# Decode attention over a 65,536-row cache: the first 192 rows of the last V tile in three pieces instead of four

## The chip, the cores and the metric

The kernel runs on one core of a Trainium2 chip. The metric is the device time of one execution in microseconds. All times inside an execution are counted from the first instruction of its profiled span. The engines are called as in the profile: PE multiplies matrices (PEld loads its weights), DVE works on vectors, ACT computes functions such as exp, POOL serves here mostly as a hand that passes signals on, and SP issues nearly all loads.

## The reference

There is one query row for each of 32 heads, and 8 key/value heads of 65,536 rows with 128 numbers each, all in bf16. Four query heads share one key/value head.

```python
B, Hq, Hkv, Sq, Sk, D = 1, 32, 8, 1, 65536, 128
def reference(q, k, v):
    rep = Hq // Hkv
    k = jnp.repeat(k, rep, axis=1)
    v = jnp.repeat(v, rep, axis=1)
    scale = D ** -0.5
    scores = jnp.einsum("bhqd,bhkd->bhqk", q, k) * scale
    p = _softmax(scores, axis=-1)
    return jnp.einsum("bhqk,bhkd->bhqd", p, v)
```

K and V are 134 MB each and every number of them is used once (for four query heads). The result is tiny.

## The kernel before

**Tiles.** Each head's K and V are cut into two halves of 256 rows per partition (NT = 256, 128 partitions): a half is a tile of 128 x 256 rows of 128 numbers, 8.4 MB. `buf` is a ring with room for three tiles. One "row" below means one row in each of the 128 partitions, 32 KB in all.

**Loads.** SP issues the loads in the order of the list `tiles` (L153 to L156): both K halves of a head, then V halves of earlier heads, and at the very end the second V half of head 6 and both V halves of head 7. Before each load SP waits until the tile that had the same place in the ring is used up. Most tiles are one load. Head 7's K tiles and the last V tiles are cut into pieces with a semaphore for each piece: `BY` gives the pieces of three V tiles, and `PIECES` those of the very last one, (head 7, second half), in which this case's change lies. All loads stand on one queue and are worked off in order. L134 is the issue in the helper `load`.

**K and scores.** DVE transposes each half of a K tile in place (`turn`, L318). PE multiplies it with the queries into four banks of `sc` (block `scores`, L460). DVE takes the maximum, ACT the exponential (L244), and DVE transposes the weights into `Ew` (L323).

**V and sums.** PE's block `values` (L479 to L492) works on 32 rows per turn (STEP): it takes one count of the semaphore `sV` (`take`, L224: wait for one, subtract one) and issues 8 matmuls of 4 rows each into `psum_o` (L484), each with its own weights from `Ew`. The counts of `sV` are given by SP for whole tiles (L168), and for the tiles in `BY` and the first `MOVED` pieces of the last tile by POOL (L216 to L218): POOL waits for each piece's landing in order and adds the number of its turns, `n // STEP`. So a piece of 64 rows gives two turns when it has landed as a whole.

**The order on PE at the end.** After head 6's second half PE closes the sum (`summed`, L501), then runs head 7's first half (64 matmuls), goes over `values_done`, `turn` and `late`, where the number of turns for the rest of the last tile is set from `sum(PIECES[:MOVED])` (192 rows), and back into `values` for these 192 rows: 6 turns, 48 matmuls. Then it goes over `values_done` (L494 to L497) and `second_done` (L499) and branches into the block `tail` (L524).

**The tail.** The pieces behind the first `MOVED` are worked off there: the first of them (44 rows) in 11 matmuls that are spread over four column groups of the array, so that four run beside one another (L533); then `psum_o` is closed (L421), DVE picks out the sum from it (L331); meanwhile PE multiplies the last 20 rows one by one into `misc` (L542) as pieces of 8, 8 and 4 land, adds what DVE picked (L431), ACT scales it (L262) and stores it (L236). Each of these pieces has a wait of its own on PE.

Nothing waits for the matmuls of the last tile but the tail itself: no later load needs its place in the ring.

Of the kernel before, what the change touches and what calls it, by code (L numbers as in the profile page):

```python
# [24 lines left out]
N = 2  # L25
FAR = 2.0 ** 126
STEP = 32
PIECES = (64, 64, 32, 32, 44, 8, 8, 4)
MOVED = 4


@with_exitstack
def kernel(
# [19 lines left out]
    assert B_ == 1 and Sq == 1 and D_ == D and Hkv == G and Hq == G * H  # L53
    assert Sk == 2 * NT * P and sum(PIECES) == NT
    SCALE = float(D) ** -0.5
# [40 lines left out]
    def sem(name):  # L96
        sems.append(nc.alloc_semaphore(name))
        return sems[-1]
# [3 lines left out]
    sL = [sem(f"sL{x}") for x in range(sum(map(len, BY.values())))]  # L102
    sP = [sem(f"sP{x}") for x in range(len(PIECES))]
    sQ = sem("sQ")
# [27 lines left out]
    def load(at, src, s, lo=0, n=NT):  # L132
        at = at % 3 * half + lo * D
        return sp.dma_start(  # L134
            out=buf[:, at:at + n * D], in_=src[:, s * half + lo * D:s * half + (lo + n) * D]
        )
# [21 lines left out]
    for at, (kind, h, s) in enumerate(tiles):  # L158
# [16 lines left out]
        elif (h, s) == (G - 1, 1):  # L175
            lo = 0
            for n, land in zip(PIECES, sP):
                load(at, vr[h], s, lo, n).then_inc(land, 16)
# [36 lines left out]
    pool.wait_ge(vit, NT // STEP * (2 * G - 4))  # L215
    for at, (land, n) in enumerate(list(zip(sL, sum(BY.values(), ()))) + list(zip(sP, PIECES))[:MOVED]):  # L216

# [196 lines left out]
    def add(reg, n, op=ALU.add):  # L414
        pe.reg_alu(reg, reg, n, op)
# [102 lines left out]
    with block("late"):  # L518

        pe.reg_alu(r_e, r_g, 4 * (sum(PIECES[:MOVED]) - NT), ALU.mult)  # L520
        add(r_e, 2048 - 4 * G * (sum(PIECES[:MOVED]) - NT))
        pe.br("values")

    with block("tail"):  # L524
        at = sum(PIECES[:MOVED])
        left = list(zip(PIECES, sP))[MOVED:]
        own = (2 * G * 2 - 1) % 3 * half
# [60 lines left out]
```

## Time and profile before

| | us |
|---|---|
| median of three runs | 628.2 |
| lowest and highest | 627.85 and 628.54 |
| the profiled execution | 628.39 |
| its span, from the first to the last instruction | 626.5 |
| PE busy in the span | 504.5 |
| DVE busy | 331.4 |
| ACT, POOL busy | 21.1, 6.0 |
| HBM read | 268.44 MB, 429 GB/s over the span |

The span is what the rows of the trace show; the 1.9 us beside it lie before the first and after the last instruction of the program. PE's rows in order of time are matmuls, and their ends are modelled; the starts are what to go by. "Idle before" is the engine's idle time just ahead of a row, with what ended it. PEq and POOLq are the queues of the engines: the waits, register operations and branches that the engine works through between its instructions. A landing is the moment at which a load's last part is signalled; the profile gives it as time from the issue. The row PEclk and the column of that name give the clock that PE was granted, as a share of full speed.

### The profile page before, as it was taken

The numbers are of one execution on the slowest core, as the hardware profiler recorded it, in microseconds if no ns is written. First come the engines' busy times: TensorE is split into PE (matmuls) and PEld (weight loads), VectorE is DVE, ScalarE is ACT, GpSimd is POOL, SyncE is SP. The second block draws the span as 40 slices with busy tenths as digits, with TensorE's granted clock in tenths as the row PEclk, the third lists the DMA queues.
The fourth block names the chain that finished last, engine by engine and source line by source line (L and its number), as shares of the span: only waits on it lengthen the run. The fifth ranks groups of instructions, "written<-read, shape, count | busy, mean of one in ns | idle before, by whom it ended". The sixth has DMA issues, their size and how long they took to land. (4 is left out here: it accounts for less than half of the span.)

```text
span 626.5 us, 8015 instructions
## 1 busy us (share of the span) xinstructions
PE 504.5 (81%) x2186; PEld 204.2 (33%) x2186; DVE 331.4 (53%) x109; ACT 21.1 (3%) x28; POOL 6.0 (1%) x16
## 2 busy tenths in 40 slices
PE   0587299798994889948799397993979988799997
PEld 0232043243331333313333133331433333333333
DVE  3983895789214892148821588215872389410100
ACT  1000100100010000100001000010000100001000
POOL 2000000000000000000000000000000000000000
PEclk9998589799998789988899889997899998999999
DMA  9999999999999999999999999999999999999997
GB/s 371 433 469 402 469 402 469 402 460 410 452 418 423 448 402 469 402 469 402 469 402 469 402 469 402 469 402 469 402 464 406 418 425 429 435 435 435 423 431 319
DMA packets 6857, 268.46 MB, mean 429 GB/s; under 512 B 840, under 2 KB 968, under 8 KB 1224
## 3 DMA queue, kind: packets, MB, share of 16 engines
q1 hardware_dynamic: 6768, 268.44, 99.4%
q10 hardware_dynamic: 88, 0.02, 0.0%
q14 instruction: 1, 0.01, 0.0%
HBM read 268.44 MB, written 0.01 MB: 429 GB/s over the span
## 5 line engine op out<-in xcount | busy, mean ns | idle before, releaser
L318 DVE STREAM_TRANSPOSE buf<-buf 128x8192 f32<-128x8192 f32 x32 | 277.2, 8694 | 87.2 <-DVEq L224 87.2
L460 PE MATMUL sc<-buf,zeros 128*128 x1024 | 247.8, 401 | 0.0
L484 PE MATMUL psum_o<-buf,Ew 128*16 x1008 | 226.0, 382 | 11.7 <-PEq L224 11.0
L460 PEld LDWEIGHTS sc<-buf,zeros 128*128 x1024 | 102.3, 100 | 137.7 <-issue 41.6
L484 PEld LDWEIGHTS psum_o<-buf,Ew 128*16 x1008 | 89.3, 89 | 145.2 <-issue 54.9
L418 PE MATMUL sc<-zeros 128*128 128x512 bf16 x32 | 13.8, 432 | 87.8 <-PEq L224 87.8
L331 DVE TENSOR_REDUCE o_r<-psum_o 128x128 f32<-128x512 f32 x10 | 6.9, 688 | 100.2 <-DVEq L224 72.4
L327 DVE COPY o_r<-o_r 4x1 f32<-4x1 f32 x9 | 1.3, 142 | 79.7 <-DVEq L224 65.6
L418 PEld LDWEIGHTS sc<-zeros 128*128 128x128 bf16 x32 | 3.1, 98 | 97.1 <-issue 96.0
L244 ACT ACTIVATE zeros<-sc,nmb 128x2048 bf16<-128x2048 f32 x8 | 15.7, 1967 | 535.9 <-DVE nmb L382 535.9
L323 DVE STREAM_TRANSPOSE Ew<-zeros 128x1024 bf16<-128x1024 bf16 x18 | 22.3, 1240 | 14.0 <-PE psum_o L484 14.0
L504 PE MATMUL misc<-each,same 128*128 128x512 f32 x18 | 11.3, 712 | 8.6 <-PEq L224 8.6
L370 DVE TENSOR_REDUCE mx<-sc 128x1 f32<-128x2048 f32 x8 | 18.0, 2253 | 0.0
L441 PE MATMUL misc<-Ew 32*128 32x128 bf16 x1 | 0.3, 283 | 10.7 <-DVE Ew L308 10.7
L208 POOL TENSOR_TENSOR zeros<-qx,quad 128x64 bf16<-128x64 bf16 x8 | 2.4, 294 | 486.6 <-ACT o_out L251 480.4
L504 PEld LDWEIGHTS misc<-each,same 128*128 128x128 f32 x18 | 2.9, 202 | 8.9 <-issue 8.8
L421 PE MATMUL sc<-zeros 128*128 128x1 bf16 x32 | 5.2, 163 | 0.0
L418 PE MATMUL psum_o<-rows,zeros 4*128 4x512 bf16 x10 | 4.5, 451 | 0.0
L289 DVE CAST Ew<-ident 32x128 bf16<-32x128 f32 x1 | 3.0, 2984 | 2.7 <-POOL ident L193 2.7
L421 PEld LDWEIGHTS sc<-zeros 128*128 128x128 bf16 x32 | 3.0, 95 | 3.9
L251 ACT ACTIVATE o_out<-psum_f,o_r 4x128 bf16<-4x128 f32 x9 | 3.1, 345 | 29.3 <-DVE o_r L337 29.3
L431 PE MATMUL psum_f<-o_r,sel 128*4 128x129 f32 x18 | 3.9, 302 | 0.0
(32 smaller groups left out, 31.9 us busy)
## 6 DMA issues: line engine op xcount, KB each, us to landing
buf<-in_k_dram SPq DMA_DIRECT2D x8, 4096.0 KB, 28.5
buf<-in_v_dram SPq DMA_DIRECT2D x5, 4096.0 KB, 32.5
buf<-in_v_dram SPq DMA_DIRECT2D x4, 2048.0 KB, 36.4
buf<-in_v_dram SPq DMA_DIRECT2D x2, 1024.0 KB, 38.7
buf<-in_v_dram SPq DMA_DIRECT2D x1, 1408.0 KB, 42.6
buf<-in_v_dram SPq DMA_DIRECT2D x2, 256.0 KB, 40.6
buf<-in_k_dram SPq DMA_DIRECT2D x12, 34.6
buf<-in_v_dram SPq DMA_DIRECT2D x12, 34.4
```

The lines of the kernel that those rows point to most:

```text
L244: act.activation(out=E[:, :], in_=sc[:, :], func=ACT.Exp, bias=nmb[:, 0:1], scale=SCALE, accum_out=o_r[:, D:D + 1],).then_inc(exd, 1)
L251: act.activation(out=o_out[:, at:at + D], in_=psum_f[0:H, 0:D], func=ACT.Copy, scale=rl).then_inc(outs, 1)
L318: dve.transpose(out=kv, in_=kv).then_inc(kt, 1)
L323: return dve.transpose(out=Ew[:, at], in_=E[:, at])
L331: return dve.tensor_reduce(out=o_r[:, 0:D], in_=psum_o[:, :].rearrange("p (y d) -> p d y", y=4), axis=AX.X, op=ALU.max)
L370: after(dve.tensor_reduce(out=mx[:, :], in_=sc[:, :], axis=AX.X, op=ALU.max))
L418: return pe.matmul(out=bank, lhsT=lhsT, rhs=rhs, start=True, stop=False)
L421: return pe.matmul(out=bank[:, 0:1], lhsT=zer[:, 0:P], rhs=zer[:, 0:1], start=False, stop=True)
L431: return pe.matmul(out=out[0:H, 0:n], lhsT=sel[:, :], rhs=o_r[:, 0:n], start=start, stop=True)
L460: pe.matmul(out=bank, lhsT=moved(wq[:, m * SLIDE + 4 * n:][:, 0:P], slide), rhs=moved(T[:, n, m // 2, m % 2], keys), start=False, stop=False,)
L484: last = pe.matmul(out=psum_o[0:16, :], lhsT=moved(Ew[:, column(4 * j + 3):][:, 0:16], weight), rhs=moved(buf[:, 4 * j * D:][:, 0:4 * D], ...
L504: pe.matmul(out=misc[:, :], lhsT=same[:, :], rhs=each[:, :].unsqueeze(1).broadcast_to([P, 16, 32]), start=True, stop=True,).then_inc(pes, 1)
```

## The change

`PIECES` cuts the last tile's 256 rows. Its first four entries, which POOL announces and the block `values` works off, become three: 96, 64 and 32 rows instead of 64, 64, 32 and 32. Their sum stays 192 rows. `MOVED`, the number of these entries, goes from 4 to 3. The four pieces behind them, 44, 8, 8 and 4 rows, stay.

```diff
-PIECES = (64, 64, 32, 32, 44, 8, 8, 4)
-MOVED = 4
+PIECES = (96, 64, 32, 44, 8, 8, 4)
+MOVED = 3
```

By this SP issues seven loads for the tile instead of eight, POOL has three landings to pass on instead of four, with 3, 2 and 1 turns instead of 2, 2, 1 and 1, and there is one semaphore less in `sP`. PE's instructions, DVE's and ACT's are the same ones, apart from the semaphores' numbers.

## Prediction

> **What bounds the kernel now.** I read the page first: the engine shares and the forty slices, then the chain that ended last, then the order of time on PE and SP over the last 50 us, and at the end single stretches with their granted clock.
>
> ```profile
> span 626.5 us, 8015 instructions
> PE 504.5 (81%) x2186; PEld 204.2 (33%) x2186; DVE 331.4 (53%) x109; ACT 21.1 (3%) x28; POOL 6.0 (1%) x16
> PEclk9998589799998789988899889997899998999999
> DMA  9999999999999999999999999999999999999997
> HBM read 268.44 MB, written 0.01 MB: 429 GB/s over the span
> ```
>
> The DMA row is full in every slice but the last: the kernel is a stream of loads, and everything before the last tile hides under it. So the change can only be worth what it moves behind the last landings. The profiled execution took 628.39 us, 1.9 us around its span; the median of the runs is 628.2, 0.2 less. I add my difference to the median.
>
> The chain that ended last, from the issue of the pieces on (start, duration, what):
>
> ```profile
> 577.63 0.33 SPq L134
> ...
> 578.00 0.43 SPq L134
> ...
> 578.48 0.43 SPq L134
> ...
> 579.43 42.63 DMA buf<-in_v_dram
> 622.06 0.04 issue
> 622.10 0.82 PE psum_o L533 x11
> 622.92 0.11 PE psum_o L421
> 623.03 1.27 PE misc L542 x20
> 624.31 0.23 PE misc L431 x2
> 624.54 0.02 issue
> 624.56 0.36 ACT o_out L262
> ```
>
> The load issued at 579.43 is the fifth piece, 44 rows. It lands at 622.06; PE begins it 0.04 us later (L533), and from there only PE and ACT follow one another to the end. So today the stream sets the end: PE waits for the 44 rows. The question is whether PE would still be the one that waits. PE in order of time, the idle time before a row in brackets:
>
> ```profile
> 594.94 14.05 PE L484 MATMUL psum_o<-buf,Ew 128*16 x64
> 610.01 3.71 PE L484 MATMUL psum_o<-buf,Ew 128*16 x16 [1.01 <-PEq L224]
> 614.02 7.14 PE L484 MATMUL psum_o<-buf,Ew 128*16 x32 [0.30 <-PEq L224]
> 622.10 0.82 PE L533 MATMUL psum_o<-buf,Ew 128*16 128x512 bf16 x11 [0.94 <-DMA buf<-in_v_dram]
> ```
>
> PE ends the tile before at 608.99. The first piece (64 rows, 16 matmuls) starts at 610.01, pieces two to four (128 rows, 32 matmuls) run without a break from 614.02 to 621.16, and then PE has 0.94 us to spare. That is the slack in which the change must fit.
>
> **The change part by part.** *Loads.* Seven transfers instead of eight, the same 256 rows in the same order on the one queue. SP issues one transfer less; the issues lie 31 to 43 us ahead of the landings, so an earlier issue buys nothing. The landings of the first three pieces, counted from their issue at 577.63, 578.00 and 578.48:
>
> ```profile
> DMA to landing us min/median/max: 31.1/31.1/31.1
> ...
> DMA to landing us min/median/max: 35.7/35.7/35.7
> ...
> DMA to landing us min/median/max: 37.7/37.7/37.7
> ```
>
> So 64 rows are there at 608.7, 128 at 613.7 and 160 at 616.2. No row shows a 96-row transfer: its landing is bounded by these two, and I take the middle, 611.2, since the engines move the same bytes in the same order. The 44 rows come at 622.06 as before, or up to 0.1 earlier without one transfer's overhead (an estimate; it costs or gains nothing once PE is late).
>
> *Hand-over.* POOL passes a landing on through L218 and PE takes it at L224. One wait less stands on POOL; what is queued behind it there are only the same waits for later pieces. From the landing at 613.7 to PE's start at 614.02 is 0.3 us, 0.35 before rounding of the landing. So the 96 rows start at 611.2 + 0.35 = 611.55, where today 64 rows start at 610.01 and 64 more at 614.02. PE's wait grows from 1.01 to 611.55 - 608.99 = 2.55 us, in one piece.
>
> *Matmuls.* None is added or removed: 192 rows are 48 matmuls at L484. The run of 32 gives (7.14 - 0.38) / 31 = 0.218 us from start to start, 0.38 being the last one's own length. The new second piece ends where the old third one did, at 160 rows: it is there at 616.2, before PE has done 96 rows (611.55 + 24 x 0.218 = 616.8). The last 32 rows follow it some 2.5 us later (616.2 - 613.7 for 32 rows), when PE still has 64 to do, so PE runs through: the last of the 48 starts at 611.55 + 47 x 0.218 = 621.8.
>
> ```profile
> L499 PEldq COMPARE_BRANCH  x1: 213/213/213, 621.1 to 621.1; - x1
> ```
>
> *Way into the tail.* After the last matmul's start (620.78 today) PE's queue goes through L494 to L499 and branches into the block at L524. That branch begins at 621.1 and takes 0.21 us, so the tail could begin at about 621.33: 0.55 us after the last start. Today this lies under the wait for the 44 rows. After the change the tail begins at 621.8 + 0.55 = 622.35 instead of 622.10: +0.25 us, if nothing else happens. The cover of 0.94 us is gone.
>
> *The granted clock.* This is the step on which the forecast turns. The page's PEclk row has dips. Stretches of 3.41 us, laid on the edges at which the clock changes in this trace (PE, PEld, DVE, ACT and POOL busy, then clock, DMA share and GB/s):
>
> ```profile
> 37.81:41.23 3.42, 1.48 (x8) 0.57 (x6) 3.35 (x1) 0.00 (x0) 0.00 (x0) 1.00 0.91 393
> 41.23:44.64 3.41, 3.18 (x14) 1.44 (x15) 2.48 (x1) 0.00 (x0) 0.00 (x0) 1.00 1.29 557
> 222.13:225.55 3.42, 1.41 (x9) 0.53 (x7) 3.42 (x2) 0.00 (x0) 0.00 (x0) 1.00 1.33 575
> 225.55:228.96 3.41, 3.41 (x9) 1.19 (x10) 3.41 (x1) 0.00 (x0) 0.00 (x0) 0.50 0.80 346
> 228.96:232.37 3.41, 3.41 (x17) 1.52 (x16) 3.41 (x1) 0.00 (x0) 0.00 (x0) 1.00 0.71 308
> 454.24:457.65 3.41, 1.44 (x8) 0.55 (x6) 3.41 (x2) 0.00 (x0) 0.00 (x0) 1.00 1.20 519
> 457.65:461.06 3.41, 3.29 (x15) 1.50 (x16) 3.41 (x1) 0.00 (x0) 0.00 (x0) 1.00 0.93 404
> 542.99:546.40 3.41, 0.54 (x3) 0.34 (x4) 3.40 (x3) 0.00 (x0) 0.00 (x0) 1.00 0.72 308
> 546.40:549.81 3.41, 3.41 (x10) 1.10 (x9) 0.43 (x2) 0.00 (x0) 0.00 (x0) 0.50 1.05 452
> 607.84:611.25 3.41, 2.40 (x12) 0.88 (x11) 0.00 (x0) 0.00 (x0) 0.00 (x0) 1.00 1.04 442
> ```
>
> A stretch with PE busy for 1.44 or 1.48 us is followed by full clock; with 1.41 or 0.54 by half the clock, for one stretch, and a busy stretch restores it. So about 2.0 us idle within one stretch costs half the clock in the next. Today the stretch from 607.84 is busy for 2.40: no dip. With the 64 rows at 610.01 gone from it, 611.25 - 610.01 = 1.24 of this falls away, 1.16 is left, and 611.25 to 614.67 would run at half clock. Whether the edges lie like that in another execution the trace cannot tell. If they may lie anywhere, 2.55 us of idle time puts 2.0 or more into one stretch in (3.41 + 2.55 - 2 x 2.0) / 3.41 = 0.57 of the cases.
>
> What a dip costs: half of 3.41 at most, 1.7 us of PE work. This row shows it on a run of 64 matmuls of the same line, and an undisturbed one stands above (594.94, 14.05):
>
> ```profile
> 545.86 15.66 PE L484 MATMUL psum_o<-buf,Ew 128*16 x64 [3.04 <-PEq L224]
> ```
>
> 15.66 - 14.05 = 1.61 us. I take 1.6. Where the dip begins before 611.55, part falls on idle time and it costs down to 1.3; I take off 0.05 for that. While the matmuls run slowly, PE's queue gets ahead, so the way into the tail (0.55) shrinks to the plain distance of two matmuls, 0.22. Sum with a dip: 621.8 + 1.6 - 0.05 + 0.22 = 623.57, against 622.10: +1.45 us. From there the chain is as today, all pieces having landed; what little PE waits for the last three now is won back, at most 0.1. So +1.4: 628.2 + 1.4 = 629.6.
>
> The Trainium skill ("TensorE: Matmul & The Clock Gate", What's actually happening) describes a free-running window of 3413 ns that doesn't start with the kernel. The trace agrees with its length (222.13 to 225.55); that the phase is free no run here shows yet.
>
> **The rivals.** *No dip.* The edges cut the 2.55 us so that neither side holds 2.0. Then only the +0.25 is left, less up to 0.1: 628.4, no change that can be told. For it speaks that 2.55 is not far above 2.0; against it that the edges of the profiled execution would give the dip. The decision lies at 2.0 us idle in a stretch, so an earlier landing helps: if the 96 rows were announced by 610.6 there could be no dip at all, but 608.7 and 613.7 leave little room for that.
>
> The Trainium skill, same page (HAM oscillation — how this bites in real kernels), gives the rule as no idle gap over about 3.4 us; by it 2.55 us would be harmless and the time 628.4. The trace disagrees: the stretch 222.13:225.55 had 2.0 us idle and half the clock followed.
>
> *The tail is slow to start.* The branch into the tail ends at 621.3 and the wait until 622.10 could hide more than it, for instance instructions that are not there yet. The bound is what the wait hides: 622.10 - 621.33 = 0.8 us more. Without a dip 628.4 + 0.8 = 629.2, still within 0.2% but nearly out of it; with a dip the queue is ahead and part of it is hidden again, 629.6 to 630.2. Against it speaks that the queue that loads instructions moved one packet in the whole span:
>
> ```profile
> q14 instruction: 1, 0.01, 0.0%
> ```
>
> *Late 96 rows.* If the transfer is announced only at 613.7, the upper bound, all 48 matmuls start 2.5 us later; at 612.3 and later it is slower by over 0.2% even without a dip. Nothing in the profile suggests it; I count it with the slow tail.
>
> *Faster.* One transfer less ends the stream up to 0.1 us sooner, 628.1. PE is then late all the same, so a gain over 0.2% (1.26 us) has no mechanism here; a little is left for what I don't see.
>
> **How the numbers follow.** A median of three with 0.57 each is a dip in 0.57² x (3 - 2 x 0.57) = 0.60. I give the dip 0.62, no dip 0.30, the slow tail or late rows 0.05, a gain 0.03. 0.2%, about what a measurement of this kernel can tell from no change, is 1.26 us, and the dip's +1.4 stands just above it, from +1.1 (it costs 1.3) to +1.6 (it costs 1.7 and nothing is won back): of its 0.62 I put 0.51 above and 0.11 below. Slower 0.51 + 0.05 = 0.56, same 0.30 + 0.11 = 0.41, faster 0.03. The range takes in both: no dip less 0.3 for the spread of the runs (627.85 to 628.54), 628.1, and the dip's +1.6 with 0.2 for the spread, 630.0. The dip's own range is 629.2 to 630.0.
>
> **What would show it.** L484 in one run of 48 matmuls from about 611.55 with 2.5 us idle ahead of it; half the clock for 3.41 us within 611 to 616; L533 starting without a wait for DMA, at about 622.35 without a dip and 623.6 with one; the landing of the 44 rows still at 622.0. Wrong would be: full clock with 2 us idle in one stretch; L533 still released by the DMA, which would mean that the 96 rows landed well ahead of 611; or a first L533 more than 0.6 us after the last L484 began.

## The result, and the profile after

The changed kernel takes 629.46 us in the median of 15 runs (628.18 to 631.44), the kernel before 627.92 us in 15 runs beside it (627.80 to 628.54): +1.5 us, a ratio of 1.0023 with a 95% interval of 1.0015 to 1.003. 629.6 us was forecast, slower by a little over 0.2%. What stands out beside the median is the spread: 3.3 us for the changed kernel, 0.7 us for the one before.

The page of the changed kernel, whose profiled execution took 629.48 us:

```profile
span 627.6 us, 8013 instructions
PE 503.7 (80%) x2186; PEld 204.1 (33%) x2186; DVE 331.5 (53%) x109; ACT 21.1 (3%) x28; POOL 6.0 (1%) x16
PEclk9989599898998889988999788997989999999998
DMA  9999999999999999999999999999999999999996
```

PE has as many instructions as before. The span is 1.1 us longer in this pair of executions, and 1.88 us lie outside it, as before. The chain that ended last no longer reaches a load (start, duration, what):

```profile
611.10 0.22 issue
611.32 11.78 PE psum_o L484 x46
623.10 0.02 PE psum_o L533 x3
...
623.53 0.65 PE psum_o L533 x5
624.18 0.11 PE psum_o L421
624.29 1.21 PE misc L542 x20
625.50 0.23 PE misc L431 x2
625.73 0.02 issue
625.75 0.36 ACT o_out L262
```

From the start of the 96 rows on, PE follows PE to the end. PE in order of time, with idle time ahead of a row in brackets:

```profile
594.15 14.19 PE L484 MATMUL psum_o<-buf,Ew 128*16 x64 [0.34 <-PEq L224]
611.32 11.78 PE L484 MATMUL psum_o<-buf,Ew 128*16 x46 [2.98 <-PEq L224]
622.73 0.39 PE L533 MATMUL psum_o<-buf,Ew 128*16 128x512 bf16 x3
622.93 0.38 PE L484 MATMUL psum_o<-buf,Ew 128*16 x1
622.94 0.39 PE L533 MATMUL psum_o<-buf,Ew 128*16 128x512 bf16 x3
623.15 0.38 PE L484 MATMUL psum_o<-buf,Ew 128*16 x1
623.16 1.02 PE L533 MATMUL psum_o<-buf,Ew 128*16 128x512 bf16 x5
624.11 0.18 PE L421 MATMUL psum_o<-zeros 128*128 128x1 bf16 x1
```

PE waits 2.98 us in one piece; then 48 matmuls go through without a wait, and no row of the tail waits for a load. The 48 take 11.83 us from the first start to the last (611.32 to 623.15). The same kernel in stretches of 3.41 us, laid on the edges at which the clock changes in this execution (PE, PEld, DVE, ACT and POOL busy, clock, DMA share, GB/s):

```profile
608.87:612.28 3.41, 0.96 (x5) 0.52 (x6) 0.00 (x0) 0.00 (x0) 0.00 (x0) 1.00 0.98 418
612.28:615.69 3.41, 3.41 (x10) 1.10 (x8) 0.00 (x0) 0.00 (x0) 0.00 (x0) 0.50 0.93 394
615.69:619.11 3.42, 3.42 (x18) 1.41 (x16) 0.00 (x0) 0.00 (x0) 0.00 (x0) 1.00 1.04 436
```

One stretch is busy for 0.96 us, and PE runs the next at half the clock, 10 matmuls in it instead of 18. That is the forecast's picture. Whether it is the cause is what the experiments are for: PE is also late, one transfer is gone, and a transfer has a new size.

### The profile page after: what moved, and what is told of

Read it like the earlier page. It is cut to its first block, busy times and chain, and to the rows that moved or that the text cites. A ratio compares the mean times of both kernels' runs of the same rounds, so it can differ in the third digit from the quotient of the medians.

```text
span 627.6 us, 8013 instructions
## 1 busy us (share of the span) xinstructions
PE 503.7 (80%) x2186; PEld 204.1 (33%) x2186; DVE 331.5 (53%) x109; ACT 21.1 (3%) x28; POOL 6.0 (1%) x16
## 5 line engine op out<-in xcount | busy, mean ns | idle before, releaser
L484 PE MATMUL psum_o<-buf,Ew 128*16 x1008 | 225.7, 381 | 13.9 <-PEq L224 13.2
L484 PEld LDWEIGHTS psum_o<-buf,Ew 128*16 x1008 | 89.1, 88 | 147.5 <-issue 57.9
L421 PE MATMUL sc<-zeros 128*128 128x1 bf16 x32 | 5.2, 163 | 0.0
L421 PEld LDWEIGHTS sc<-zeros 128*128 128x128 bf16 x32 | 3.0, 95 | 3.9
```

The costliest lines, as they stand in the source:

```text
L421: return pe.matmul(out=bank[:, 0:1], lhsT=zer[:, 0:P], rhs=zer[:, 0:1], start=False, stop=True)
L484: last = pe.matmul(out=psum_o[0:16, :], lhsT=moved(Ew[:, column(4 * j + 3):][:, 0:16], weight), rhs=moved(buf[:, 4 * j * D:][:, 0:4 * D], ...
```

## The experiments

**Two ways of announcing the same loads.** Eight loads as before, cut 64, 32, 64, 32. In one kernel each is announced when it lands; in the other POOL announces the first two together when the second has landed, as the 96-row load does.

```diff
-PIECES = (64, 64, 32, 32, 44, 8, 8, 4)
+PIECES = (64, 32, 64, 32, 44, 8, 8, 4)
```

The joint announcement has this as well, in POOL's loop at L216:

```diff
+        if land is sP[0]:
+            pool.wait_ge(land, 32)
+            continue
+        if land is sP[1]:
+            n += PIECES[0]
-        pool.wait_ge(land, 32 if land is sP[0] else 16).then_inc(sV, n // STEP)
+        pool.wait_ge(land, 16).then_inc(sV, n // STEP)
```

> The same eight loads, cut 64, 32, 64, 32, each announced when it lands, so PE starts on 64 rows at once and has no idle time of 2 us in one stretch. Halved clock: as before, within 0.3 us, little spread. If the order of the piece sizes matters by itself: as the joint announcement.

Measured: 627.98 us (627.84 to 628.54), the same as the kernel before in the same runs (627.98); ratio 0.9999 (0.999 to 1.0008). Its PE rows:

```profile
609.66 5.46 PE L484 MATMUL psum_o<-buf,Ew 128*16 x24 [1.01 <-PEq L224]
616.20 5.39 PE L484 MATMUL psum_o<-buf,Ew 128*16 x24 [1.07 <-PEq L224]
621.78 0.82 PE L533 MATMUL psum_o<-buf,Ew 128*16 128x512 bf16 x11 [0.19 <-DMA buf<-in_v_dram]
```

The idle time is in two parts of 1.0 us, and the tail still waits for the 44 rows.

> Eight loads as before, cut 64, 32, 64, 32; POOL announces the first two together, as three turns, when the 32 rows have landed. If only the moment of the announcement counts (2.5 us of idle time in one piece, then half the clock in most executions): as the changed kernel, +1.2 to +1.7 us, with times spread from +0.3 to +3. If the 96-row load itself or the number of loads matters: as before, within 0.3 us.

Measured: 629.51 us (628.33 to 629.84), ratio 1.0019 (1.001 to 1.0028). Its PE rows and two of its stretches:

```profile
611.60 11.78 PE L489 MATMUL psum_o<-buf,Ew 128*16 x46 [2.65 <-PEq L229]
```

```profile
608.27:611.69 3.42, 0.77 (x5) 0.17 (x2) 0.00 (x0) 0.00 (x0) 0.00 (x0) 1.00 1.02 429
611.69:615.10 3.41, 3.41 (x9) 1.13 (x9) 0.00 (x0) 0.00 (x0) 0.00 (x0) 0.50 1.05 447
```

The loads of the two kernels are the same to the byte; a wait on POOL makes 1.5 us. So neither the 96-row transfer nor the number of transfers is what costs, but the moment at which PE hears of the rows. Whether it costs by PE's late start or by the clock, these two kernels alone don't tell.

**One load less, joined elsewhere.** Seven loads, cut 64, 64, 64.

```diff
-PIECES = (96, 64, 32, 44, 8, 8, 4)
+PIECES = (64, 64, 64, 44, 8, 8, 4)
```

> Seven loads as in the changed kernel, but 64, 64, 64: the two last pieces are joined, not the first two. PE waits 1.0, 0.3 and about 1.2 us ahead of the pieces, at no place 2.0 us in a stretch of 3.41 us: full clock. It starts the last 16 matmuls at about 618.7 and reaches the tail at about 622.5 where the 44 rows land at 621.8: +0.5 to +0.8 us by lateness alone. If a load less costs 1.5 us wherever it is: +1.5 us.

Measured: 628.82 us (628.53 to 629.02), ratio 1.0013 (1.0004 to 1.0022): +0.8 us with a spread of 0.5.

```profile
609.75 3.71 PE L484 MATMUL psum_o<-buf,Ew 128*16 x16 [1.01 <-PEq L224]
613.76 3.64 PE L484 MATMUL psum_o<-buf,Ew 128*16 x16 [0.29 <-PEq L224]
618.65 3.64 PE L484 MATMUL psum_o<-buf,Ew 128*16 x16 [1.25 <-PEq L224]
622.46 0.82 PE L533 MATMUL psum_o<-buf,Ew 128*16 128x512 bf16 x11 [0.17 <-issue]
```

This is lateness without a halved clock: in this profile the clock is full from 549.57 us to the end of the span. The 44 rows were issued at 578.69 and landed 43.0 us later:

```profile
DMA to landing us min/median/max: 43.0/43.0/43.0
```

That is 621.7, and L533 starts 0.8 us after it. Lateness has a price of its own, then, but it is the same in every execution and doesn't spread.

**Keeping PE busy in the wait.** The changed kernel, with matmuls that nobody reads in PE's idle time: a block that is entered from `late` the second time only, and writes an unused PSUM bank `warm`. Loads and announcements stay.

```diff
-        pe.br("values")
+        pe.br_eq(g, G + 1, on_true="keep", on_false="values")
+    with block("keep"):
+        for _ in range(7):
+            pe.matmul(out=warm[:, :], lhsT=zer[:, 0:P], rhs=zer, start=True, stop=True)
+        pe.br("values")
```

> The changed pieces (96, 64, 32), with seven matmuls of zeros into a PSUM bank that nothing reads, put on PE between the tile before and the wait for the 96 rows (7 x 0.22 = 1.5 us of the 2.5 to 3 us in which PE was idle). Loads and announcements stay as in the changed kernel. If the halved clock makes the change slow: no stretch with 2.0 us idle is left, full clock from 607 us to the end, and only PE's late start remains, +0.1 to +0.4 us on the kernel before. If PE's late start, the one load less or a slow way into the tail makes it slow: as the changed kernel, +1.5 us.

Measured: 629.34 us (628.17 to 629.70), ratio 1.0018 (1.0009 to 1.0027). By the device time this spoke against the clock. Two variants asked whether zeros count as work, one with V rows and weights, one with V rows and zero weights:

```diff
-            pe.matmul(out=warm[:, :], lhsT=zer[:, 0:P], rhs=zer, start=True, stop=True)
+            pe.matmul(out=warm[0:16, :], lhsT=Ew[:, 12:28], rhs=buf[:, 0:4 * D], start=True, stop=True)
```

> As the kernel with seven matmuls of zeros in PE's idle time, but the seven multiply V rows and weights of the tile before (16 columns, 512 wide, as L484 does), into the PSUM bank that nothing reads. If the clock gate counts work on data and not the zeros, and the halved clock is what makes the change slow: no halving in any execution, 628.1 to 628.7 us with little spread, +0.1 to +0.6. If the halved clock is not the cause, or something other than idle time halves it here: spread from 628.2 to 629.8 and a median about 629.4, as with the zeros.

> The same seven matmuls with V rows as moving data and zeros as weights. If moving data alone counts as activity: as with data and weights, 628.1 to 628.7 us. If products or weights are needed: as with zeros, a median about 629.4.

Measured: 629.10 us (628.45 to 629.68) with data, ratio 1.0016 (1.0007 to 1.0025), and 629.30 us (628.35 to 630.04) with zero weights, ratio 1.0018 (1.0009 to 1.0027). No difference between the three. The kernel with zeros was profiled once more:

> The kernel with seven matmuls of zeros once more, for a profile of an execution with the longer time. If zeros don't count as activity, half the clock follows a stretch that PE's rows show as busy but for about 1 us; if they count, the clock stays full and the longer time must show somewhere else.

Measured: 628.5 us in its one execution, so not one with the longer time. Its PE rows:

```profile
608.97 1.68 PE L526 MATMUL warm<-zeros 128*128 128x512 bf16 x7 [0.63 <-PEq L225]
611.30 10.69 PE L485 MATMUL psum_o<-buf,Ew 128*16 x48 [0.65 <-PEq L225]
622.19 0.82 PE L538 MATMUL psum_o<-buf,Ew 128*16 128x512 bf16 x11 [0.20 <-issue]
```

The 48 matmuls are back at 10.69 us, and none of the four profiles with seven such matmuls has a halved clock between 600 us and the end of its span, though two of them, with data and with zero weights, are of executions with the longer time (629.27 and 629.20 us). What told more was the span that each execution lists beside its device time; that it would be the measure was not said before these runs, and the loop below tests the same on the device's clock:

```
                           executions  span, median (range)       outside the span, median
before, beside the first four      33  626.1  (625.9 to 626.8)    1.90
changed                            15  627.6  (626.3 to 629.6)    1.87
joint announcement                 11  627.6  (626.4 to 627.9)    1.91
each announced                     11  626.1  (625.9 to 626.6)    1.92
64, 64, 64                         11  626.9  (626.7 to 627.1)    1.87
seven of zeros                     11  626.6  (626.3 to 627.1)    2.69
seven with data                    11  626.6  (626.2 to 627.0)    2.73
seven, zero weights                11  626.6  (626.2 to 626.8)    2.76
```

Inside the span the matmuls do what the clock theory says: none of 33 executions is above 627.1, where the changed kernel has its median at 627.6. The seven matmuls cost 0.8 us again outside the span. The two profiles with the longer time, 2.83 and 2.62 us outside, show where: in both, a packet of 16 KB on an instruction queue moves some 1.9 us after the last instruction (DMA of 626 to 632 us, with data and with zero weights):

```profile
q8 instruction: 1, 0.02, 1.2%
q8 instruction: 1, 0.02, 1.1%
```

The other ten profiles have no packet there and at most 2.2 us outside. So the extra time lies behind the last instruction and goes with this packet, as far as two profiles can show it. Two kernels separate it from the question:

```diff
 # the branch that is never taken
-        pe.br_eq(g, G + 1, on_true="keep", on_false="values")
+        pe.br_eq(g, G - 1, on_true="keep", on_false="values")
 # the loop
+        pe.reg_mov(r_s, 0)
         pe.br_eq(g, G + 1, on_true="keep", on_false="values")
     with block("keep"):
-        for _ in range(7):
+        for _ in range(2):
             pe.matmul(out=warm[:, :], lhsT=zer[:, 0:P], rhs=zer, start=True, stop=True)
-        pe.br("values")
+        add(r_s, 1)
+        pe.br_lt(s, 3, on_true="keep", on_false="again")
+    with block("again"):
+        pe.br("values")
```

> The kernel with seven matmuls of zeros, but the branch to them is never taken: the same length of code on PE, nothing in the idle time. The three kernels with such matmuls had spans of at most 627.1 us and yet 629.1 to 629.3 us of device time: 2.7 us outside the span instead of 1.9. If the length of the code is behind that: about 2.7 us outside here too, and spans as the changed kernel's (627.6 in the median, since the halved clock is back), so about 630.2 us. If running the matmuls is behind it: 1.9 us outside and about 629.5.

Measured: 629.66 us (628.97 to 629.90), ratio 1.0023 (1.0014 to 1.0032). The median span is 627.6, as the changed kernel's: with the idle time open again, the halved clock is back (in its profile from 612.11 on). Outside the span the median is 2.0 us, with 2.85 and 3.1 in two of 11. So the length of the code alone seldom does it, while with the seven matmuls run more than 2.4 us lie outside in 21 of 33 executions; why stays open.

> The idle time filled from a short loop, three turns of two matmuls of zeros (ten instructions of PE more than the changed kernel, instead of sixteen). Halved clock: no span over 627.2 us, median 626.5. If the time outside the span goes with the length of the code, it lies between 1.9 and 2.7 us and the device time between 628.4 and 629.2; if it stays 1.9, 628.4 us, which would show the same on the clock of the device.

Measured: 628.29 us (628.12 to 629.09), ratio 1.0004 (0.9995 to 1.0013); median span 626.3 (626.2 to 627.2), 1.89 outside. Its PE rows and stretches:

```profile
609.80 1.47 PE L527 MATMUL warm<-zeros 128*128 128x512 bf16 x6 [0.72 <-PEq L225]
611.51 10.70 PE L485 MATMUL psum_o<-buf,Ew 128*16 x48 [0.25 <-PEq L225]
622.38 0.82 PE L542 MATMUL psum_o<-buf,Ew 128*16 128x512 bf16 x11 [0.17 <-issue]
```

```profile
608.22:611.63 3.41, 2.44 (x11) 0.66 (x9) 0.00 (x0) 0.00 (x0) 0.00 (x0) 1.00 0.93 399
611.63:615.05 3.42, 3.42 (x17) 1.33 (x16) 0.00 (x0) 0.00 (x0) 0.00 (x0) 1.00 1.04 446
```

This is the same on the device's clock: the changed kernel's loads, announcements and lateness, six useless matmuls, and the loss falls from 1.5 to 0.25 us, which these runs can't tell from none. The halved clock is the cause of the rest.

**The changed kernel once more.**

> The changed kernel once more, for another position of the stretches' edges. If the halving follows 2.0 us idle within one stretch: either half the clock from about 611 to 615 us and +1.1 to +1.7, or, where the edge cuts the idle time, full clock and at most +0.6.

Measured: 629.37 us, 2.63 us idle ahead of the 96 rows, half the clock from 611.31 to 614.72. No execution of it without the halving was caught in a profile. That there are such is read from the spans alone: 4 of 15 lie at 626.3 to 626.8, where the loop's lie, 8 at 627.4 to 627.8, and 3 above (628.2, 628.6, 629.6).

No kernel here beats the one before: it waits for the stream at the end, and so does the best of these, with each piece announced.

## Why the prediction was right, step by step

The mechanism was the forecast one: one long wait, half the clock in the next stretch, a tail that no longer waits for a load. That 629.6 and 629.46 us lie only 0.14 apart is partly luck. The time to which the difference was added, 628.2, is 0.3 us above the 627.92 of the same kernel beside the changed one, and the difference was +1.5 instead of +1.4. The forecast range held the case without a dip too, so the time alone would not have decided; the stretches and the loop do.

- **Loads.** Right. The 44 rows landed at 621.76 here against 622.06 before, in an execution whose whole stream was 0.3 us ahead. The 96 rows were taken at 611.2, between bounds of 608.7 and 613.7; they landed at 610.98 (issued at 575.98, 35.0 us before). The "up to 0.1" for one transfer less had no row behind it; the landings bear it out, for two pieces of 32 rows took 4.97 us from landing to landing before, and one of 64 rows 4.89 us in the kernel with 64, 64, 64. The 96 rows:

```profile
DMA to landing us min/median/max: 35.0/35.0/35.0
```

- **Hand-over and idle time.** 611.55 was forecast for PE's start, 611.32 measured. The idle time was forecast as 2.55 us and was 2.98, since PE ended the tile before at 608.34 instead of 608.99. The reason lies 60 us earlier: in the execution that the prediction was made from, a halved clock (546.40 to 549.81) had lengthened a run of 64 matmuls to 15.66 us, here it took 14.23. The other profiles with the halving have 2.63, 2.65 and 2.97. All twelve profiles agree with the reason: PE ends that tile at 608.65 to 609.07 in the seven with the halved clock near 546 us, and at 608.23 to 608.36 in the five without.

```profile
545.56 14.23 PE L484 MATMUL psum_o<-buf,Ew 128*16 x64 [3.03 <-PEq L224]
```

- **Way into the tail.** Right. Without the halving, 622.35 was forecast and the loop kernel begins at 622.38, 0.55 us after the last L484's start (611.51 + 10.70 - 0.38 = 621.83). So nothing more than the branch was hidden there, and the rival of a slow tail falls; that of late 96 rows falls with their landing at 610.98. Counted from the landing of the 44 rows, at 621.92 in the loop's execution, the tail is 0.46 us late where 0.29 was forecast; the device time shows +0.25 all the same.
- **Price of the dip.** Right in size: 1.6 us was taken; the 48 matmuls need 11.83 us from first start to last in the changed kernel and 10.32 in the loop's, 1.5 more. Between the median spans of the two lie 1.3 us.
- **Entry with a dip.** Here the step was wrong in kind, without moving the sum: L533 was to begin 0.22 us after the last L484. Its first matmul starts at 622.73, 0.42 us ahead of the last L484, and the two mix. It gains nothing, for the sum is closed at 624.11, where 623.57 + 0.75 (L533 to L421 before) less the 0.3 by which the stream is ahead gives 624.02.
- **How often.** Mis-sized: 0.57 was forecast. If spans of 627.3 and more are counted as dips, they are 11 of 15 in the changed kernel, 8 of 11 with the joint announcement and 8 of 11 with the branch that is never taken: 27 of 37, 0.73. The terms that were off are the idle time and a little the limit: with the 2.63 to 2.98 us of the four profiles and 1.95 the same formula gives from (3.41 + 2.63 - 3.9) / 3.41 = 0.63 to (3.41 + 2.98 - 3.9) / 3.41 = 0.73. Thirty-seven executions can't tell these apart.
- **Edges.** That they lie differently in each execution holds: stretches begin at 607.84 in the profile before, and at 608.87 (changed kernel), 608.27 (joint announcement) and 608.22 (loop). Over all twelve profiles the edges spread over 3.0 of the 3.41 us. So the median moved by 1.5 us, and a single execution may show nothing. By the rule of the Trainium skill ("TensorE: Matmul & The Clock Gate", HAM oscillation — how this bites in real kernels) of no idle gap over about 3.4 us, which the prediction set against the rows, the changed kernel would have stayed at 628.4. The traces disagree: 2.65 and 2.98 us of idle time were followed by half the clock.

What stays open: the three executions of the changed kernel with spans of 628.2, 628.6 and 629.6 us. A dip that begins while PE still waits may last a second stretch, which would fit the size of the longest, but no profile shows one at this place.

## What to carry to other kernels

Before merging pieces at the end of a load-bound kernel, look at what the engine behind them does with the longer wait: idle time that cost nothing by itself can cost clock afterwards, at the one place where no slack is left to hide it. Lay the trace out in stretches on the edges of the granted clock, find how much idle time in one stretch was followed by half of it, and keep each wait near the end under that; work done in smaller announcements, or even a few useless matmuls, does so. Where a change makes the spread of the times grow from 0.7 to 3 us, look for something that depends on chance in time, and compare spans as well as totals.

## What the runs showed of the hardware

- The limit is about 1.95 us idle in a stretch of 3.41 us, and it is not sharp by PE's rows, whose ends are modelled: 1.44 us busy was followed by full clock in the profile before, and 1.48 by half in this one (second profile of the kernel with zeros). Over all twelve profiles, after their first 30 us, a stretch at full clock was followed by half the clock from 1.92 us idle on, and by full clock up to 1.99.

```profile
145.93:149.34 3.41, 1.48 (x7) 0.71 (x8) 3.41 (x2) 0.00 (x0) 0.00 (x0) 1.00 0.71 308
149.34:152.75 3.41, 3.41 (x10) 1.17 (x9) 3.41 (x1) 0.00 (x0) 0.00 (x0) 0.50 1.33 577
```

- How busy a stretch at half the clock must be to restore it, PE's rows don't tell. In the changed kernel one with 0.3 us idle left the next at half; in the loop kernel one with 0.76 us idle was followed by full clock. The first holds 5 matmuls, the second 7:

```profile
62.73:66.15 3.42, 3.10 (x5) 0.69 (x5) 1.78 (x3) 0.00 (x0) 0.00 (x0) 0.50 1.42 613
66.15:69.56 3.41, 0.00 (x0) 0.00 (x0) 2.76 (x3) 2.30 (x3) 0.29 (x1) 0.50 0.71 308
```

```profile
205.44:208.86 3.42, 2.66 (x7) 1.03 (x8) 3.42 (x2) 0.00 (x0) 0.00 (x0) 0.50 1.41 613
208.86:212.27 3.41, 3.41 (x17) 1.46 (x16) 3.41 (x1) 0.00 (x0) 0.00 (x0) 1.00 0.71 308
```

- Matmuls of zeros on zeros keep the clock up as well as those on data: spans of 626.6 us in the median for all three kinds, against 627.6 without such matmuls.
- Matmuls of the tail start ahead of earlier ones in the queue (three at 622.73, before those of L484 at 622.93 and 623.15). The tail's eleven go round four column groups, and L484 uses the first; the six that start early are as many as lie in the other three in two rounds. That the column group decides is read from this, not tested.
- Seven more matmuls in a row on PE, run once, added 0.8 us outside the span; six, as a loop of two, added nothing. The two profiles with the longer time have a packet of 16 KB on an instruction queue after the last instruction; why it is moved is open.
